# A gated-attention kernel with experts: GpSimd's arithmetic in the attention moved to VectorE and ScalarE

## The chip, the core and the metric

The kernel runs on one core of a Trainium2 chip. Its time is device time in microseconds, the median of several executions. Besides that there is one profiled execution, with the start and length of every instruction on each engine: TensorE (PE in the profile, PEld for its weight loads), VectorE (DVE), ScalarE (ACT), GpSimd (POOL) and SyncE (SP), which issues most of the transfers. Each engine works through its own queue of instructions in order and waits at semaphores for the others.

## The reference

Four sequences of 768 positions, eight heads of 48 channels, go through a linear attention whose state decays by a complex gate. After it a router sends each of the 3072 tokens to one of eight experts.

```python
mag = np.sqrt(a_re * a_re + a_im * a_im)
scale = np.minimum(mag, 0.999) / (mag + 1e-06)
a_re_n, a_im_n = (a_re * scale, a_im * scale)
for t in range(S):                       # S = 768
    new_re = ar * S_re - ai * S_im       # state: 48 x 48 for each batch and head
    new_im = ar * S_im + ai * S_re
    S_re, S_im = (new_re + kv, new_im)   # kv = outer product of k[t] and v[t]
    y[:, :, t] = np.einsum('bhd,bhde->bhe', q[:, :, t], S_re)
# experts, on x = y as (B*S, H*D) = (3072, 384)
logits = x @ w_gate                      # 8 experts
expert_idx = np.argmax(logits, axis=1)
h = np.maximum(x_sorted[lo:hi] @ w1[e], 0.0)     # 384 -> 1024
y_sorted[lo:hi] = h @ w2[e]                      # 1024 -> 384
return gate_w[:, None] * y
```

## The kernel before

**Two stages.** The attention takes chunks of 128 positions. A group g is one chunk of one batch (24 groups), a unit u is two groups (12 units), and four groups, one for each batch, make a step s of the sequence (6 steps). The experts follow: tokens are gathered by expert from a table in DRAM (`xs`), go through two matrix products, and are scattered to the output.

**What a unit computes.** The gate of each position is turned into a log magnitude and an angle; their running sums over a chunk come from a matmul with a triangular matrix.
- `decay_steps` (L226 to L250): ACT takes Ln of a_re (A) and Exp of its negative (R); the ratio of imaginary to real part replaces `ai` (L238); its square goes to R (L239); ACT takes Ln(1 + R), DVE forms A (L243), ACT an Exp, DVE the final A (L248).
- `decay_sums` (L269): matmul `csl` of A, then ACT makes E and Ei, the decay factor and its inverse, from PSUM.
- `angle_sums` (L298): matmul `cst` of the angles; DVE rounds it (r, L308), subtracts (f, L309) and takes the absolute value (fa, L312). `rotation` (L319) makes sine and cosine (CS) on ACT.
- `decayed` (L327): Qe = q * E and Ke = k * Ei (L333), for each group.
- `rotated` (L335): DVE multiplies these by CS into Q and K (L338).
- `scores` (L419): transposes of Q and K (tp), copies to SBUF (qt, kt; L78), scores (at), a mask (am, L438), and K^T v (dk).
- `outputs` (L448): y from the masked scores and from the state G, the new state t = dk + G (L468); once per step, all four G are t times the step's total decay M (L475). Then y goes to the expert table's rows (x) and to the router's logits.

**Routing.** Every other unit, `choose` and `route` (L352, L373) rank the tokens of four groups by expert, with some twenty DVE instructions on a few elements (L379 to L405, such as ov, rk, far, to). `put` (L407) then scatters the four groups' rows to `xs` by an indirect DMA, which GpSimd issues. `place` spreads these scatters over the units.

**Order.** The functions above are written down unit by unit with one unit's look-ahead (the gate of u + 1 beside the groups of u - 1). The order on each engine is then settled when the program is built, from dependences and estimated costs, so an instruction that moves to another engine can change the order on all. Two orders are fixed by hand: `act` chains the ACT activations in the order of the program, and `pool` does the same for GpSimd, with the scatters in the same chain:

```python
    def pool(ins):
        if "pool" in T:
            queue(ins, T["pool"])
        T["pool"] = ins
```

**Buffers that matter.** All `csl` and `cst` share one PSUM buffer (`psM`, bufs=1): each such matmul waits until the one before has been read, by E and Ei or by f. R, E and Ei have one buffer, Qe, Ke, Q and K two.

Of the kernel before, what the change touches and what calls it, by code (L numbers as in the profile page):

```python
# [13 lines left out]
AF = mybir.ActivationFunctionType  # L14
OP = mybir.AluOpType
# [14 lines left out]
def bc(ap, axis, n):  # L30

    shape = list(ap.shape)
    shape.insert(axis, n)
    return ap[tuple([slice(None)] * axis + [None])].to_broadcast(shape)
# [3 lines left out]
def kernel(  # L38
# [12 lines left out]
    nc = tc.nc  # L51
    B, H, S, D = q.shape
    DD = 2 * D
# [20 lines left out]
    def mm(o, lhsT, rhs, start=True, stop=True):  # L74
        return nc.tensor.matmul(o, lhsT=lhsT, rhs=rhs, start=start, stop=stop, skip_group_check=True)  # L75
# [10 lines left out]
    def const(shape, name, dt=FP):  # L86
        return cp.tile(shape, dt, name=name)
# [25 lines left out]
    gbuf = [const([P, H, DP], f"G{i}") for i in range(B)]  # L113
# [35 lines left out]
    T, W_T = {"put": []}, {}  # L149

    def queue(ins, before):

        tc.add_manual_dep(ins.ins, before.ins.name, NOSYNC, reason="queue order")
        return ins
# [32 lines left out]
    def act(**kw):  # L187

        ins = nc.scalar.activation(**kw)  # L189
        if "act" in T:  # L190
            queue(ins, T["act"])
        T["act"] = ins
# [6 lines that stand above are left out]
# [27 lines left out]
    def decay_steps(u):  # L226

        ar, ai = T["ar", u], T["ai", u]
        A = un.tile([P, W], FP, tag="A", name="A")
        R = un.tile([P, W], FP, tag="R", name="R", bufs=1)  # L230
        T["L", u], T["th", u] = A, ai

        def s0():
            act(out=A, in_=ar, func=AF.Ln)

        def s1():
            act(out=R, in_=A, func=AF.Exp, scale=-1.0)
            pool(nc.gpsimd.tensor_tensor(out=ai, in0=ai, in1=R, op=OP.mult))  # L238
            pool(nc.gpsimd.tensor_tensor(out=R, in0=ai, in1=ai, op=OP.mult))  # L239

        def s2():
            act(out=R, in_=R, func=AF.Ln, bias=1.0)
            nc.vector.scalar_tensor_tensor(out=A, in0=A, scalar=2.0, in1=R, op0=OP.mult, op1=OP.add)  # L243

        def s3():

            act(out=R, in_=A, func=AF.Exp, scale=-0.5, bias=ln2e6)
            nc.vector.scalar_tensor_tensor(out=A, in0=A, scalar=LN_CAP2, in1=R, op0=OP.min, op1=OP.subtract)  # L248

        return [s0, s1, s2, s3]  # L250
# [37 lines left out]
    def decay_total(s):  # L288

        mt = psL.tile([P, H, B], FP, tag="mm", padded_shape=[P, 128, B], name="mt")  # L290
        for h in range(H):
            nc.tensor.transpose(
                out=mt[0:DD, h], in_=T["er", s][:, h].rearrange("p a d -> p (a d)"), identity=ident[0:B, 0:B]
            )
        T["M", s] = un.tile([P, B, H], FP, tag="M", name="M")
        nc.scalar.copy(out=T["M", s][0:DD], in_=mt[0:DD].rearrange("p h b -> p b h"))
# [30 lines left out]
    def decayed(u, c):  # L327

        sl = slice(c * DM, (c + 1) * DM)
        for nm, src, dec in (("Q", "q", "E"), ("K", "k", "Ei")):  # L330
            e = T[nm, u, c] = ch.tile([P, H, D], FP, tag=nm + "e", name=nm + "e")
            o = e.rearrange("p h d -> p (h d)")
            pool(nc.gpsimd.tensor_tensor(out=o, in0=T[src, u][:, sl], in1=T[dec, u][:, sl], op=OP.mult))  # L333

    def rotated(u, c, nm):  # L335
        t = ch.tile([P, H, 2, D], FP, tag=nm, name=nm)
# [4 lines left out]
    def logits(xt, j):  # L341

        lt = psL.tile([P, P], FP, tag="mm", padded_shape=[P, 512], name="lt")
        for i in range(HP):
            mm(lt[32 * i : 32 * i + 32], wg[:, i], xt[:, i])
        ls = xl.tile([P, P], FP, tag="ls", name="ls")
        nc.scalar.copy(out=ls, in_=lt)
        lp = psL.tile([P, E], FP, tag="mm", padded_shape=[P, 512], name="lp")
        T["lp"] = mm(lp, ls, sel)
        nc.vector.tensor_copy(out=lg[:, j], in_=lp)  # L350
# [97 lines left out]
    def outputs(g):  # L448

        u, c = divmod(g, U)  # L450
        s, b = divmod(g, B)
        qts, ats = T.pop(("s", g))
        V, G = T["v", u][:, c], gbuf[b]
        y = psY.tile([P, HP, P], FP, tag="y", name="y")
        for i in range(HP):
            for z in range(2):
                hg, j = divmod(2 * i + z, 4)
                mm(y[z * DP : (z + 1) * DP, i], V[:, 2 * i + z], ats[hg][:, j], True, s == 0)
            if s > 0:
                for z in range(2):  # L460
                    hg, j = divmod(2 * i + z, 4)
                    mm(y[z * DP : (z + 1) * DP, i], G[0:DD, 2 * i + z], qts[hg][0:DD, j], False, True)
        if s < CB - 1:
            t = ch.tile([P, H, D], FP, tag="t", name="t")
            if s == 0:
                nc.scalar.copy(out=t[0:DD], in_=T["dk", g][0:DD])
            else:
                nc.vector.tensor_tensor(out=t[0:DD], in0=T["dk", g][0:DD], in1=G[0:DD, :, 0:D], op=OP.add)  # L468
            if b == B - 1:
                decay_total(s)  # L470
            T["t", b] = t
            if b == B - 1:
                for i in range(B):
                    M = bc(T["M", s][0:DD, i], 2, D)
                    pool(nc.gpsimd.tensor_tensor(out=gbuf[i][0:DD, :, 0:D], in0=T["t", i][0:DD], in1=M, op=OP.mult))  # L475
        xt = xl.tile([P, HP, P], FP, tag="xt", name="xt")
        nc.scalar.copy(out=xt, in_=y)
        tp = psB.tile([P, HP, 2, DP], FP, tag="tp", name="tpx")
        for i in range(HP):
            nc.tensor.transpose(out=tp[:, i].rearrange("p z d -> p (z d)"), in_=xt[:, i], identity=ident)  # L480
        if b == 0:
            T["x", g] = T["x"] = xl.tile([P, GR, XW], FP, tag="x", name="x", bufs=3)
        nc.scalar.copy(
            out=T["x"][:, b, :DM].rearrange("p (i z d) -> p i z d", z=2, d=D), in_=tp[:, :, :, 0:D]
        )
        logits(xt, g)
# [13 lines left out]
    for z in range(2):  # L500
        nc.sync.dma_start(
            out=wg[z * DP : z * DP + D, :, 0:E],
            in_=w_gate.rearrange("(i z d) e -> z d i e", z=2, d=D)[z],
# [12 lines left out]
    for u in range(NU + 1):  # L516
# [32 lines left out]
        for c in range(U):  # L549
            g = (u - 1) * U + c  # L550
            if g >= 0:
                scores(g)
            if u < NU:
                decayed(u, c)
            if g > 0:
                outputs(g - 1)
# [9 lines left out]
        if NU - 8 <= u < NU - 1:  # L566
            load_w(0, [u - (NU - 8)])
    outputs(NT - 1)
    for f in T["put"]:
        f()  # L570
# [301 lines left out]
```

## Time and profile before

| | before |
|---|---|
| time, median of 3 | 650.44 us (648.06 to 651.69) |
| span of the profiled execution | 648.4 us |
| attention | about 20 to 305 us |
| mean granted clock of TensorE | 0.962 |
| PE busy | 580.5 us (90%) |
| DVE busy | 252.0 us (39%) |
| ACT busy | 276.9 us (43%) |
| POOL busy | 209.2 us (32%) |

In the profile the first part is each engine's busy time. The second cuts the span into 40 slices of 16.2 us; a digit is the busy share in tenths, and PEclk is the clock that TensorE was granted, in tenths of full speed. A line of the timeline has start, length, engine, source line, operation, output and inputs with their shapes, and in brackets how long the engine had stood idle before it and who ended that. Every matmul has the line L75 and every plain copy L78, since helpers issue them: go by the names of the tiles. What GpSimd does in the attention:

| line | what | count | mean |
|---|---|---|---|
| L238 | ai = ai * R, 128x768 | 12 | 1811 ns |
| L239 | R = ai * ai, 128x768 | 12 | 1467 ns |
| L333 | Qe, Ke, 128x384 | 48 | 996 and 992 ns |
| L475 | G = t * M, 96x384 | 20 | 1111 ns |
| L408 | scatter to xs | 24 | 1025 ns |

### The profile page before, as it was taken

How to read it: one execution, taken by the hardware profiler on the slowest of the kernel's cores; microseconds unless marked ns; L12 is line 12 of the kernel's file. 1: busy time of each engine (PE TensorE's matmuls, PEld its weight loads, DVE VectorE, ACT ScalarE, POOL GpSimd, SP SyncE). 2: the span in 40 equal slices, each digit the busy share in tenths (PEclk: the TensorE clock that was granted, in tenths of full speed). 3: DMA queues.
4: the chain of work that ended last, by engine and by line, in shares of the span. 5: the costliest groups of instructions: out<-in, count | busy, mean ns of one | idle time of the engine just before them, and what ended most of it. 6: DMA issues, size and time to landing. Idle time of an engine off the chain costs nothing. (4 is left out here: it accounts for less than half of the span.)

```text
span 648.4 us, 8580 instructions
## 1 busy us (share of the span) xinstructions
PE 580.5 (90%) x3319; PEld 381.6 (59%) x3319; DVE 252.0 (39%) x499; ACT 276.9 (43%) x467; POOL 209.2 (32%) x192
## 2 busy tenths in 40 slices
PE   1497998998799699799989999999999999999993
PEld 0185776766668477587776555555555555555551
DVE  2355468567755758858231211212121021211210
ACT  5566774764564466475320115152341614225100
POOL 3444144174163444533211106032140512305111
PEclk9998889889799799899999999999999999999998
DMA  9979854653544525024303543736425373430000
GB/s 184 205 233 197 196 100 87 138 129 78 122 102 96 116 46 111 14 62 174 109 25 110 201 148 117 252 109 212 138 83 201 111 258 110 155 112 24 10 12 30
DMA packets 154233, 79.74 MB, mean 123 GB/s; under 512 B 130230, under 2 KB 145735, under 8 KB 154184
## 3 DMA queue, kind: packets, MB, share of 16 engines
q1 hardware_dynamic: 147008, 69.48, 41.8%
q0 software_dynamic: 3456, 9.47, 4.3%
q10 hardware_dynamic: 3720, 0.16, 0.3%
q8 instruction: 28, 0.46, 0.3%
q14 instruction: 21, 0.17, 0.1%
HBM read 63.74 MB, written 15.98 MB: 123 GB/s over the span
## 5 line engine op out<-in xcount | busy, mean ns | idle before, releaser
L75 PE MATMUL yps<-w2t,ht 128*128 128x384 f32 (+1 forms) x512 | 147.2, 488 | 0.3 <-DVE y L639 0.3
L75 PE MATMUL hps<-xt,w1t 128*128 128x448 f32 (+2 forms) x432 | 147.0, 500 | 0.0
L75 PEld LDWEIGHTS yps<-w2t,ht 128*128 128x128 f32 (+1 forms) x512 | 81.4, 177 | 64.5 <-issue 15.0
L75 PEld LDWEIGHTS hps<-xt,w1t 128*128 128x128 f32 x432 | 79.9, 190 | 61.6 <-issue 58.7
L624 ACT ACTIVATE ht<-hps 128x448 f32<-128x448 f32 (+2 forms) x36 | 18.1, 503 | 135.8 <-PE hps L75 135.8
L606 POOL DMA_INDIRECT out_dram<-y,xg x32 | 30.9, 966 | 94.2 <-DVE y L639 44.3
L639 DVE TENSOR_SCALAR y<-yps,xg 128x384 f32<-128x384 f32 x24 | 14.8, 617 | 118.4 <-PE yps L75 118.4
L628 DVE TENSOR_SCALAR ht<-hps 128x448 f32<-128x448 f32 (+2 forms) x36 | 20.6, 573 | 103.0 <-PE hps L75 103.0
L75 PEld LDWEIGHTS at<-qt,kt 96*128 96x128 f32 x384 | 52.7, 208 | 12.5 <-ACT kt L78 4.5
L75 PE MATMUL at<-qt,kt 96*128 96x128 f32 x384 | 57.7, 298 | 2.3 <-ACT kt L78 1.7
L677 POOL TENSOR_TENSOR cs<-cs,cw 128x768 f32<-128x768 f32 x12 | 21.7, 1805 | 117.4 <-ACT cw L673 117.4
L238 POOL TENSOR_TENSOR ai<-ai,R 128x768 f32<-128x768 f32 x12 | 21.7, 1811 | 115.2 <-ACT R L189 112.5
L75 PE MATMUL y<-am,v 128*64 128x128 f32 x384 | 52.4, 294 | 0.0
L75 PE MATMUL cst<-ai,tri_turn 128*128 128x384 f32 x48 | 26.3, 635 | 25.1 <-DVE f L309 22.6
L408 POOL DMA_INDIRECT xs<-x,to x24 | 24.6, 1025 | 73.2 <-DVE x L404 31.3
L438 DVE TENSOR_TENSOR am<-at,tri 128x512 f32<-128x512 f32 x48 | 33.0, 688 | 38.8 <-PE at L75 38.7
L75 PE MATMUL y<-qt,G 96*64 96x128 f32 x320 | 45.2, 283 | 0.0
L75 PE MATMUL csl<-A,tri_half 128*128 128x384 f32 x48 | 25.2, 613 | 19.8 <-DVE A L248 17.2
L75 PEld LDWEIGHTS y<-am,v 128*64 128x64 f32 x384 | 33.0, 140 | 13.2 <-issue 8.2
L430 PE MATMUL tp<-ident,Q 128*96 128x128 f32 x192 | 34.7, 297 | 2.9 <-DVE Q L338 1.6
L75 PE MATMUL dk<-v,K 128*96 128x48 f32 x320 | 34.1, 261 | 3.4 <-DVE t L468 3.4
L78 ACT COPY qt<-tp 96x512 f32<-96x512 f32 x48 | 27.0, 580 | 21.1 <-PE tp L430 20.6
(122 smaller groups left out, 829.0 us busy)
## 6 DMA issues: line engine op xcount, KB each, us to landing
w1t<-in_moe_w_dram SPq DMA_DIRECT2D x7, 1536.0 KB
w2t<-in_moe_w_dram SPq DMA_DIRECT2D x7, 1536.0 KB
xs<-zrow SPq DMA_DIRECT2D x7, 772.0 KB
ar<-in_a_re_dram SPq DMA_DIRECT2D x12, 384.0 KB
ai<-in_a_im_dram SPq DMA_DIRECT2D x12, 384.0 KB
q<-in_q_dram SPq DMA_DIRECT2D x12, 384.0 KB
k<-in_k_dram SPq DMA_DIRECT2D x12, 384.0 KB
v<-in_v_dram SPq DMA_DIRECT2D x12, 384.0 KB
```

The source lines that it names most:

```text
L75: return nc.tensor.matmul(o, lhsT=lhsT, rhs=rhs, start=start, stop=stop, skip_group_check=True)
L78: (nc.scalar.copy if i % 2 else nc.vector.tensor_copy)(out=o, in_=in_)
L238: pool(nc.gpsimd.tensor_tensor(out=ai, in0=ai, in1=R, op=OP.mult))
L408: pool(nc.gpsimd.indirect_dma_start(out=xs[:, :], out_offset=bass.IndirectOffsetOnAxis(ap=to[:, i : i + 1], axis=0), in_=x[:, i], in_offse ...
L430: nc.tensor.transpose(out=tp[0:DD, j], in_=X[:, hg * 4 + j], identity=ident)
L438: nc.vector.tensor_tensor(out=am, in0=at, in1=bc(tri, 1, 4), op=OP.mult)
L606: return nc.gpsimd.indirect_dma_start(out=out, out_offset=bass.IndirectOffsetOnAxis(ap=idx, axis=0), in_=y[0:m], in_offset=None, bounds_ch ...
L624: relu = nc.scalar.activation(out=ht[:, f], in_=ps, func=AF.Relu)
L628: nc.vector.tensor_scalar(out=ht[:, f], in0=ps, scalar1=0.0, scalar2=None, op0=OP.max)
L639: nc.vector.tensor_scalar(out=y, in0=ps, scalar1=gate, scalar2=None, op0=OP.mult)
L677: nc.gpsimd.tensor_tensor(out=s, in0=s, in1=w, op=OP.add)
```

## The change

All four kinds of arithmetic leave GpSimd. The ratio, the products for Qe and Ke, and the state decay go to VectorE; the square becomes a Square activation on ScalarE, inside the chain of activations. GpSimd keeps the scatters of the attention, and its two instructions of the range check beside the experts are left as they are. The aim is to free VectorE and GpSimd from each other, to shorten the steps that GpSimd took, and to let the scatters go without waiting in a queue of arithmetic.

```diff
         def s1():
             act(out=R, in_=A, func=AF.Exp, scale=-1.0)
-            pool(nc.gpsimd.tensor_tensor(out=ai, in0=ai, in1=R, op=OP.mult))
-            pool(nc.gpsimd.tensor_tensor(out=R, in0=ai, in1=ai, op=OP.mult))
+            nc.vector.tensor_tensor(out=ai, in0=ai, in1=R, op=OP.mult)
+            act(out=R, in_=ai, func=AF.Square)
...
-            pool(nc.gpsimd.tensor_tensor(out=o, in0=T[src, u][:, sl], in1=T[dec, u][:, sl], op=OP.mult))
+            nc.vector.tensor_tensor(out=o, in0=T[src, u][:, sl], in1=T[dec, u][:, sl], op=OP.mult)
...
-                    pool(nc.gpsimd.tensor_tensor(out=gbuf[i][0:DD, :, 0:D], in0=T["t", i][0:DD], in1=M, op=OP.mult))
+                    (nc.vector.tensor_tensor(out=gbuf[i][0:DD, :, 0:D], in0=T["t", i][0:DD], in1=M, op=OP.mult))
```

The instruction order changes with it. On VectorE, in a unit that routes, the new order is: Qe and Ke of the first group, x, ai (L238), ov, rk, far, far, am, to, Qe and Ke of the second group, r, f, r, A (L243), f, am, fa, A (L248). On ScalarE the Square stands between Exp (R) and the second pair of E and Ei. On TensorE the next unit's first `csl` comes after the second `cst`, with half a group of transposes and eight or nine y products between them.

## The prediction

> **What bounds the kernel now.** I read the page's first two parts, then the busy time of each engine in stretches of a few microseconds, then the waits of the attention, and last the timelines of VectorE (DVE) and GpSimd (POOL) at the places where TensorE (PE) stood still. The page first:
>
> ```profile
> PE 580.5 (90%) x3319; PEld 381.6 (59%) x3319; DVE 252.0 (39%) x499; ACT 276.9 (43%) x467; POOL 209.2 (32%) x192
> ...
> PE   1497998998799699799989999999999999999993
> DVE  2355468567755758858231211212121021211210
> POOL 3444144174163444533211106032140512305111
> PEclk9998889889799799899999999999999999999998
> ```
>
> The attention fills slices 1 to 19 (about 20 to 305 us); the experts after it have PE at 9 throughout. So only the attention can change. There PE is mostly busy but has dips, DVE stands at 5 to 8, and the granted clock falls to 7 or 8 in the slices with a dip. One dip in stretches of 2 us (columns: PE, PEld, DVE, ACT, POOL, clock, DMA):
>
> ```profile
> 157.00:159.00 2.00, 2.00 (x21) 1.16 (x21) 1.76 (x5) 0.34 (x1) 1.77 (x3) 1.00 0.01 2
> 159.00:161.00 2.00, 0.88 (x14) 0.64 (x10) 1.97 (x2) 1.94 (x4) 1.97 (x3) 1.00 0.35 74
> 161.00:163.00 2.00, 0.00 (x0) 0.00 (x0) 2.00 (x1) 0.00 (x0) 2.00 (x3) 0.82 1.18 213
> 163.00:165.00 2.00, 0.01 (x1) 0.01 (x1) 1.87 (x4) 0.00 (x0) 0.65 (x1) 0.50 0.08 8
> 165.00:167.00 2.00, 2.00 (x5) 1.39 (x6) 0.32 (x1) 0.00 (x0) 0.00 (x0) 0.50 0.03 8
> 167.00:169.00 2.00, 2.00 (x12) 1.96 (x11) 2.00 (x4) 0.86 (x2) 0.00 (x0) 0.50 0.62 126
> ```
>
> PE and ACT stop altogether, DVE is "busy" with one instruction, and PE then runs some 5 us at half clock. The DVE and POOL timelines say which instruction, and PE's what it waited for:
>
> ```profile
> 157.55 1.10 DVE L396 TENSOR_SCALAR ov<-rk 128x4 f32<-128x4 f32 x1
> ...
> 159.08 4.60 DVE L401 TENSOR_TENSOR far<-far,ov 128x4 f32<-128x4 f32 x1
> 163.72 0.16 DVE L403 SCALAR_TENSOR_TENSOR to<-far,rk 128x4 int32<-128x4 f32 x1
> 163.79 0.55 DVE L308 TENSOR_SCALAR r<-cst 128x384 f32<-128x384 f32 x1
> ```
> ```profile
> 159.82 1.00 POOL L333 TENSOR_TENSOR Qe<-q,E 128x384 f32<-128x384 f32 x1
> 160.76 1.00 POOL L333 TENSOR_TENSOR Ke<-k,Ei 128x384 f32<-128x384 f32 x1
> 161.72 0.99 POOL L333 TENSOR_TENSOR Qe<-q,E 128x384 f32<-128x384 f32 x1
> 162.66 0.98 POOL L333 TENSOR_TENSOR Ke<-k,Ei 128x384 f32<-128x384 f32 x1
> ```
> ```profile
> 164.99 1.65 PE L75 MATMUL cst<-ai,tri_turn 128*128 128x384 f32 x2 [5.11 <-DVE f L309]
> ```
>
> A DVE instruction on four elements per partition, 0.16 us elsewhere, lasts 4.60 us and ends just when POOL's run of four products ends. Behind it in DVE's queue stand r and f, which PE's second cst needs. In the waits of 20 to 305 us this is PE's main named loss:
>
> ```profile
> PE cst L75 <- DVE f L309: 22.6, 11, 5.1
> PE csl L75 <- DVE A L248: 3.6, 1, 3.6
> PE dk L75 <- DVE t L468: 3.4, 3, 1.1
> ```
>
> The same place comes once in each unit that routes: at 105, 158, 212 and 265 us.
>
> **What the Trainium skill says.** "SBUF — State Buffer", section Who interferes with whom: a DVE instruction with two SBUF inputs contends with a GpSimd instruction that reads SBUF, and the loser waits for the whole instruction. The trace agrees: 4.60 us for 0.16 us of work, four back-to-back POOL instructions long. "TensorE: Matmul & The Clock Gate", Part 1: after an idle window of about 3.4 us the clock halves. The trace agrees: 0.50 after 5.1 us of idleness. "VectorE: DVE Perf Modes", the errata section: an fp32 tensor_tensor lasts (N+151)/0.96 ns. That is 0.56 us for 384 elements and 0.96 us for 768; the trace has 0.55 (L309, L468) and 0.96 (L243).
>
> **The change part by part.**
> - L238 (angle ratio, 12 times): 1.81 us on POOL becomes about 0.96 us on DVE (L243's row).
> - L239 (its square, 12 times): 1.47 us on POOL becomes a Square on ACT, about 0.84 us (128x768 ACTIVATE rows of 0.83 to 0.85; the Square of L673 has 0.83).
> - L333 (decayed Q and K, 48 times): 0.99 us on POOL becomes 0.55 us on DVE.
> - L475 (state decay, 20 times): 1.11 us on POOL becomes about 0.55 us on DVE (L468, 96x384). One operand is broadcast; L338, also with one, has 0.95 against 0.96, so I add nothing for it.
>
> POOL loses all 109 us of work beside DVE in the attention; DVE gains 12 x 0.96 + 48 x 0.55 + 20 x 0.55 = 49 us, ACT 10 us. DVE loses its stalls: L401 is 15.0 us for 6 x 0.16, L396 4.4 for 6 x 0.17, and L397, L400 and L248 show some 3 us over their usual times: about 20 us. DVE thus goes from 184 us in the attention to about 213.
>
> Gain A, the four routing stalls. In the changed kernel's order DVE has, between the rank (L395) and r: x 0.16, ai 0.96, ov, rk, far, far 0.7, am 0.69, to 0.16, Qe and Ke 1.1: 3.8 us, against 6.2 now (157.55 to 163.79). PE's idleness of 5.1 us shrinks by about 2.5 to 3, to below what halves the clock, and the roughly 6 us at half clock (163 to 169), worth 3 us, go with it. So 5.7 us each, 4 x 5.7 = 23 us.
>
> Gain B, the decay chain. ACT waits 20.3 us, ten times, for POOL's R (L239). Two steps of 3.3 us become 0.96 + 0.84 = 1.8 us. But the Square now stands in ACT's queue in front of the second E and Ei (L276, L277), which the first cst waits for through the one PSUM buffer, and ACT waits there for DVE's ai. I count half of the 1.5 us, in 11 units: 8 us.
>
> Gain C, the state update. It lasts 3.53 + 1.47 us on POOL in each of five rounds and four times 0.55 = 2.2 on DVE; little of PE's time hangs on it (dk behind t: 3.4 us): 3 us.
>
> Cost D, a fuller DVE queue. In the new order csl (next unit) follows the second cst after only some 2.1 us of PE work (half a group of transposes, eight or nine y products), while DVE needs r, A (L243), f, am, fa and A (L248), 4.2 us, before csl may start (in the units with the state update r, K, f, A: 3.1 us). That is a wait of 1 to 2 us per unit; behind csl stand the next at and tp. Less than a full unit's 2 us everywhere, since early units have fewer PE instructions: about 1 us x 11 = 11 us. The other new DVE work lies beside PE and ACT work: per unit DVE comes to about 18 us in a unit of 24.
>
> Sum: 23 + 8 + 3 - 11 = 23; 650.4 - 23 = 627 us. The start (DMA share near 1 until 50 us) and the experts stay; the scatters alone on POOL leave earlier, but each needs DVE's index or gate first, and they are hidden.
>
> **The rivals.**
> - The new order costs nothing (D is zero, because PE's own queue covers it): 34 us gained, 616 us; if clock dips outside the four stalls (slices at 8 before 100 us) also go, down to 606. For it: PE's waits other than cst's are small now. Against it: DVE's queue gets 49 us longer.
> - Half a gain: the routing stretch on DVE keeps PE idle over 3.4 us, and the clock still halves; A is only 2.5 x 4 = 10, B, C and D as above: 10 us, 640 us. For it: 3.8 us of DVE work in one piece, in front of r.
> - Slower: DVE becomes the bound. If half of its new 49 us stand in PE's way (24), and A brings only its idle part (10 to 12), B and C nothing, it ends 12 us slower, 662. For it: each unit's r, f, fa, A and the products for Q and K all pass one in-order queue. Against it: 213 us in 260 to 285 leave a fifth to a quarter of it free, and stalls of 20 us are gone for certain.
> - No change: gains of A and losses of D cancel, about 650.
>
> **How the numbers follow.** Likeliest, 627 (617 to 636): 0.45. D nothing or less: 0.25. Half gain: 0.16. No change: 0.04. Slower: 0.10. So faster 0.86, same 0.04, slower 0.10. Range: from 608, which takes in most of the D-nothing case, to 644, which takes in the half gain; outside are the full clock at the low end (about 0.06) and no change and slower (0.14).
>
> **What would show it.** Right: L401 and L396 at 0.16 us; no gaps of 5 us before the second cst; the clock at 1.0 where POOL used to run; DVE near 210 us before the experts, who start some 23 us earlier and last as before. The L333 and L475 products at 0.55, L238 at 0.96. D right: new PE waits of 1 to 2 us on A (L248) before csl. Wrong: PE waits on DVE in every unit that sum to more than now, ACT waiting for ai longer than it did for POOL, or products on DVE longer than 0.6 us.

## The result and the profile after

| | before | after |
|---|---|---|
| time, median of 4 runs | 649.73 us (648.06 to 651.69) | 621.82 us (620.54 to 622.01) |
| span of the profiled execution | 648.4 us | 618.8 us |
| mean granted clock of TensorE | 0.962 | 0.988 |
| first expert product (`hps`) starts at | 328.3 us | 297.5 us |

The ratio of after to before is 0.9565, with a 95% interval of 0.9534 to 0.9597. A few executions ran longer at a lower granted clock than the others of their kernel; the ratios leave them out, and only_state below, with three of four such, has no usable ratio. Of the 29.6 us between the two spans, the attention brings 30.8 and the experts give 1.2 back. The page's first two parts, after:

```profile
PE 563.5 (91%) x3319; PEld 369.7 (60%) x3319; DVE 264.6 (43%) x579; ACT 284.5 (46%) x479; POOL 104.0 (17%) x100
...
PE   1498799899899899998899999999999999999993
...
DVE  2567787787787779781312112121121211211111
...
POOL 1000000100200200302120042140521405214011
PEclk9999999999999999999799999999999999999997
```

PE has the same 3319 matmuls in 17 us less of busy time, since a matmul at half clock is busy for longer (the second pair of `cst` took 1.65 us at a clock of 0.50 in the prediction's line; at full clock such a pair takes 0.88). PEclk has lost its dips of the attention and has a new one in slice 19, where the experts begin. DVE holds 80 instructions more, which take 48.9 us, but only 12.6 us more busy time: some 25 us of stalls are gone, and records of neighbouring instructions overlap a little, which busy time counts once. The dip that the prediction showed has this counterpart, again in stretches of 2 us:

```profile
147.00:149.00 2.00, 2.00 (x21) 1.83 (x18) 1.89 (x6) 1.60 (x4) 0.00 (x0) 1.00 0.37 75
149.00:151.00 2.00, 2.00 (x21) 1.11 (x21) 1.35 (x5) 0.90 (x3) 0.00 (x0) 1.00 0.84 139
151.00:153.00 2.00, 1.90 (x20) 1.39 (x19) 0.96 (x3) 1.92 (x5) 0.00 (x0) 1.00 1.14 230
```

PE (first column after the length) hardly pauses, POOL (fifth) is empty, and the clock stays at 1.00. In the same place, DVE's timeline:

```profile
147.72 0.16 DVE L396 TENSOR_SCALAR ov<-rk 128x4 f32<-128x4 f32 x1
...
148.31 0.16 DVE L401 TENSOR_TENSOR far<-far,ov 128x4 f32<-128x4 f32 x1
...
149.16 0.55 DVE L333 TENSOR_TENSOR Qe<-q,E 128x384 f32<-128x384 f32 x1
149.63 0.55 DVE L333 TENSOR_TENSOR Ke<-k,Ei 128x384 f32<-128x384 f32 x1
150.83 0.56 DVE L308 TENSOR_SCALAR r<-cst 128x384 f32<-128x384 f32 x1 [0.65 <-PE cst L75]
```

L401 took 4.60 us before and takes 0.16 now. Before `r`, DVE now even waits 0.65 us for PE. What PE still waits for up to 285 us, where the attention's last units run:

```profile
PE tp L430 <- DVE Q L338: 6.8, 5, 1.5
PE csl L75 <- DVE A L248: 5.8, 9, 3.5
PE y L75 <- DVE am L438: 3.4, 5, 0.8
PE cst L75 <- DVE f L309: 3.0, 4, 1.2
```

The wait of `cst` for f has fallen from 22.6 us to 3.0; others on DVE have grown.

**A ledger for all runs.** From 20 us to the first expert product, one line of the windows view gives length, PE's busy time and clock. Here for before, then after:

```profile
20.00:328.20 308.20, 268.64 (x2276) 208.79 (x2277) 192.45 (x367) 179.63 (x307) 123.31 (x110) 0.93 0.53 119
```
```profile
20.00:297.30 277.30, 249.76 (x2275) 195.47 (x2275) 203.03 (x442) 184.98 (x314) 22.69 (x20) 0.99 0.59 132
```

Length less PE busy is idle time: 39.6 and 27.5 us. One minus the clock (0.928 and 0.993 unrounded), times the length, is what the clock cost: 22.2 and 1.9. The rest is work at full clock: 247 and 248. It stays at 246 to 252 us in every kernel below (262 in the one with added matmuls), so a kernel's time is this work, plus idle, plus clock. Two limits of this ledger: where PE is idle while the clock is halved, the time stands in both columns (2.7 us in before, 1.9 in ratio_only, about 1 in after and decay_stays, less elsewhere). And the clock's record begins only at 37 to 41 us. Up to there a `cst` matmul takes 0.85 us against 0.49 later, so PE ran at not much over half speed; about 6 us of this are part of the "work" of every kernel (5.5 to 7.0).

The table has this ledger and, as "DVE stalls", what DVE instructions took above the shortest of their own line and shape, where that is more than 0.1 us. Each row is one profiled execution, and executions differ: in the largest group, before ran with mean clocks of 0.960 to 0.978 and took 644 to 650 us. Each group of runs had runs of before beside it, with medians of 647 to 649 us.

| kernel | median us | `hps` starts | PE idle | lost to the clock | DVE stalls, the most at |
|---|---|---|---|---|---|
| before | 647 to 650 | 328.2 | 40 | 22.2 | 24.9, L401 14.1 |
| ratio_only | 650.2 | 328.5 | 42 | 20.5 | 24.1, L400 12.9 |
| only_state | not used | 321.7 | 40 | 11.9 | 26.5, L381 9.1 |
| rank_psum | 639.3 | 315.2 | 35 | 8.5 | 14.8, L243 8.2 |
| warm12 | 639.0 | 316.6 | 29 | 5.5 | 24.8, L396 12.8 |
| only_products | 638.0 | 316.8 | 31 | 17.1 | 19.2, L381 10.4 |
| square_only | 628.5 | 308.0 | 35 | 3.4 | 22.3, L381 11.6 |
| decay_stays | 626.3 | 304.1 | 25 | 11.3 | 22.0, L333 14.6 |
| after | 621.8 | 297.3 | 28 | 1.9 | 0 |
| both_dve | 621.4 | 298.0 | 22 | 6.8 | 20.2, L381 8.9 |
| after_early | 618.4 | 296.5 | 26 | 0 | 0 |
| only_decay | 617.2 | 295.3 | 27 | 1.7 | 8.7 |
| state_stays | 617.0 | 294.0 | 25 | 0 | 3.0 |
| products_stay | 616.2 | 292.2 | 25 | 0 | 16.4, L475 6.7 |

### The profile page after: what moved, and what is told of

The parts are those of the page before. It is cut to its first block, busy times and chain, and to the rows that moved or that the text cites. A ratio compares the mean times of both kernels' runs of the same rounds, so it can differ in the third digit from the quotient of the medians.

```text
span 618.8 us, 8535 instructions
## 1 busy us (share of the span) xinstructions
PE 563.5 (91%) x3319; PEld 369.7 (60%) x3319; DVE 264.6 (43%) x579; ACT 284.5 (46%) x479; POOL 104.0 (17%) x100
## 5 line engine op out<-in xcount | busy, mean ns | idle before, releaser
L408 POOL DMA_INDIRECT xs<-x,to x24 | 26.6, 1107 | 284.4 <-DMA fl<-f 109.4
L639 DVE TENSOR_SCALAR y<-yps,xg 128x384 f32<-128x384 f32 x24 | 14.8, 617 | 118.4 <-PE yps L75 118.4
L75 PE MATMUL at<-qt,kt 96*128 96x128 f32 x384 | 53.5, 282 | 0.8 <-ACT kt L78 0.7
L75 PEld LDWEIGHTS at<-qt,kt 96*128 96x128 f32 x384 | 47.9, 192 | 10.2 <-DVE kt L78 3.1
L75 PE MATMUL y<-am,v 128*64 128x128 f32 x384 | 50.6, 285 | 3.5 <-DVE am L438 3.4
L75 PE MATMUL y<-qt,G 96*64 96x128 f32 x320 | 42.9, 278 | 0.0
L75 PE MATMUL csl<-A,tri_half 128*128 128x384 f32 x48 | 24.2, 590 | 20.5 <-DVE A L248 17.9
L75 PEld LDWEIGHTS y<-am,v 128*64 128x64 f32 x384 | 31.6, 135 | 14.4 <-issue 7.7
L78 ACT COPY qt<-tp 96x512 f32<-96x512 f32 x48 | 27.5, 583 | 21.5 <-PE tp L430 21.3
L430 PE MATMUL tp<-ident,K 128*96 128x128 f32 x192 | 30.8, 279 | 1.5 <-DVE K L338 1.5
L75 PE MATMUL dk<-v,K 128*96 128x48 f32 x320 | 32.2, 253 | 0.0
```

Source lines behind the costliest of these rows:

```text
L78: (nc.scalar.copy if i % 2 else nc.vector.tensor_copy)(out=o, in_=in_)
L408: pool(nc.gpsimd.indirect_dma_start(out=xs[:, :], out_offset=bass.IndirectOffsetOnAxis(ap=to[:, i : i + 1], axis=0), in_=x[:, i], in_offse ...
L430: nc.tensor.transpose(out=tp[0:DD, j], in_=X[:, hg * 4 + j], identity=ident)
L639: nc.vector.tensor_scalar(out=y, in0=ps, scalar1=gate, scalar2=None, op0=OP.mult)
```

## The experiments

The theory from the prediction is that DVE's stall behind POOL's products holds PE up and then halves its clock. Against it stand the length of the decay step (two slow POOL instructions in it), and the order: where POOL's work falls in each unit.

### One part alone, and all but one part

The change has three parts: decay (L238, L239), products (L333) and state (L475). Each was made alone on the kernel before (only_...) and undone alone in the kernel after (..._stays).

only_products:
```diff
-            pool(nc.gpsimd.tensor_tensor(out=o, in0=T[src, u][:, sl], in1=T[dec, u][:, sl], op=OP.mult))
+            nc.vector.tensor_tensor(out=o, in0=T[src, u][:, sl], in1=T[dec, u][:, sl], op=OP.mult)
```


> Only the products for Qe and Ke (L333) go to DVE; ratio, square and state decay stay on GpSimd. Theory: GpSimd's run of four products is what stalls DVE, so most of the 28 us is here: 628 to 636, L401 under 1 us. Rival (each part brings its share of the shorter chain): about a third, 640.

Measured: 637.95 us, ratio 0.9834 (0.9788 to 0.988): outside what the theory said, and close to the rival's third (640). L401 is at 0.16 us, the gaps of 5 us are gone, but the clock still costs 17.1 us. The stall moved to L381 (cx) and to the products themselves, now on DVE: at 154.35 us two cx instructions take 1.85 us together and the next 1.32 while POOL runs L238 (1.80) and L239 (1.47) from 154.19 us. Removing POOL work from one place does not free DVE where other POOL work remains.

only_decay:
```diff
-            pool(nc.gpsimd.tensor_tensor(out=ai, in0=ai, in1=R, op=OP.mult))
-            pool(nc.gpsimd.tensor_tensor(out=R, in0=ai, in1=ai, op=OP.mult))
+            nc.vector.tensor_tensor(out=ai, in0=ai, in1=R, op=OP.mult)
+            act(out=R, in_=ai, func=AF.Square)
```


> Only ratio and square (L238, L239) leave GpSimd; products and state decay stay there. Theory: the run of four products remains, so L401 or a neighbour still lasts 2 us or more on average, and little is gained: 640 to 650. Rival (chain, since this is the step that ACT waited for): 630 to 638.

Measured: 617.21 us, ratio 0.9519 (0.9475 to 0.9562), far below both expectations. POOL keeps all 48 products, and yet L401 is at 0.16 us in all six places. POOL's timeline of this kernel in a unit that routes shows why:

```profile
142.11 1.00 POOL L333 TENSOR_TENSOR Qe<-q,E 128x384 f32<-128x384 f32 x1 [5.81 <-ACT E L189]
143.08 1.71 POOL L333 TENSOR_TENSOR Ke<-k,Ei 128x384 f32<-128x384 f32 x1
148.17 1.00 POOL L333 TENSOR_TENSOR Qe<-q,E 128x384 f32<-128x384 f32 x1 [3.39 <-DVE am L438]
149.13 1.00 POOL L333 TENSOR_TENSOR Ke<-k,Ei 128x384 f32<-128x384 f32 x1
```

The run of four products has become two pairs, 3.4 us apart, and L401, at 145.31 us, falls between them.

products_stay and state_stays, on the kernel after:
```diff
-            nc.vector.tensor_tensor(out=o, in0=T[src, u][:, sl], in1=T[dec, u][:, sl], op=OP.mult)
+            pool(nc.gpsimd.tensor_tensor(out=o, in0=T[src, u][:, sl], in1=T[dec, u][:, sl], op=OP.mult))
```
```diff
-                    (nc.vector.tensor_tensor(out=gbuf[i][0:DD, :, 0:D], in0=T["t", i][0:DD], in1=M, op=OP.mult))
+                    pool(nc.gpsimd.tensor_tensor(out=gbuf[i][0:DD, :, 0:D], in0=T["t", i][0:DD], in1=M, op=OP.mult))
```


> The changed kernel with the products for Qe and Ke (L333) back on GpSimd. Theory: DVE instructions with two SBUF inputs stall again for up to 4 us in the units that route, the clock dips come back: 636 to 648. Rival (chain): the ratio and square are short and off GpSimd, 622 to 630.

> The changed kernel with the state decay (L475) back on GpSimd. The parts do not add: with ratio and square off GpSimd the rest is worth nothing, so 616 to 623. If the state decay on DVE is worth what it brought together with the products (11 us between only_products and decay_stays): 630 to 634.

Measured: products_stay 616.22 us, ratio 0.9513 (0.9481 to 0.9545), the lowest median of all, where the theory had it among the slow ones and the rival, too, expected more (622 to 630); state_stays 616.97 us, 0.9494 (0.9416 to 0.9573), as foretold. The windows view of products_stay, up to its first expert product:

```profile
20.00:292.20 272.20, 247.53 (x2276) 194.85 (x2277) 198.40 (x397) 186.29 (x317) 72.08 (x66) 1.00 0.61 135
```

POOL is busy for 72 us and DVE has 16.4 us of stalls, but PE has a clock of 1.00 and less idle time than in the kernel after. So the products did not have to move. It reaches the experts 5.1 us earlier than after does. At the same transposes of `xt` (tpx) it is 2.9 us ahead at 208 us and 2.3 us ahead at 287 us; the rest comes at the handover to the experts (see after_early below). What gained the first part was not traced.

decay_stays (products and state moved, decay left on POOL) and only_state:

> The changed kernel with ratio and square back on GpSimd; the products and the state decay stay on DVE. If moving ratio and square is what brings the gain, and the rest almost nothing, 634 to 642. If the products and the state decay bring most when they move together, 622 to 630.

> Only the state decay (L475) goes to DVE. The ratio, the square and the four products stay on GpSimd back to back, so the stall of L401 or a neighbour stays: 642 to 650. If the state update is what costs (PE waits for dk behind t): 632 to 640.

Measured: decay_stays 626.26 us, 0.9661 (0.9611 to 0.9711), in the second range: products and state bring more when they move together. only_state is inconclusive (ratio 1.0152, from 1.0031 to 1.0274); the one execution that counts took 643.8 us. Together: none of the parts 647, products 638, decay 617, products and state 626, decay and products or decay and state 616 to 617, all three 622. The parts don't add. Decay alone brings 30 us, products alone 9, and on top of decay neither brings anything that can be told from noise.

### The stall without the change: rank_psum

The ranking's small tiles rk and far go to PSUM, so that none of the four instructions from ov to the second far (L396 to L401) has two SBUF inputs. PE, ACT and POOL keep exactly the order of before; on DVE a small instruction of the ranking changes places with its neighbour in a few spots.

```diff
-        ps = psL.tile([P, n + 1, E], FP, tag="mm", padded_shape=[P, 64, E], name="rps")
+        ps = psL.tile([P, n + 3, E], FP, tag="mm", padded_shape=[P, 64, E], name="rps")
...
-        rk = xl.tile([P, n], FP, tag="rk", name="rk")
+        rk = ps[:, n + 1, 0:n]
...
-        far = xl.tile([P, n], FP, tag="far", name="far")
+        far = ps[:, n + 2, 0:n]
```


> The kernel before, with the rank and its distance (rk, far) kept in PSUM, so that ov, rk, far and far (L396 to L401) have at most one SBUF input each; GpSimd keeps all its arithmetic, and the order on every engine is that of before. Theory (the stall behind GpSimd's products is the main cost): L401 falls from 2.5 us to about 0.2 us, the 5 us gaps before the second cst fall to 1 or 2 us, the clock stays up in these units, and it gains 12 to 20 us (630 to 638), unless the next DVE instruction with two SBUF inputs, A (L243), takes over the stall. Rival (the gain is that of shorter steps once GpSimd is out of the chain): under 4 us gained, 646 to 650.

Measured: 639.3 us (636.46 to 647.89), ratio 0.9866 (0.9798 to 0.9934). L401 fell from 2.51 us on average to 0.16, but the gain is 8 us, not the whole: the exception that the expectation named came true. The DVE timeline in the third routing unit of this kernel:

```profile
253.91 0.56 DVE L309 TENSOR_TENSOR f<-cst,r 128x384 f32<-128x384 f32 x1
254.39 4.54 DVE L243 SCALAR_TENSOR_TENSOR A<-A,R 128x768 f32<-128x768 f32 x1
```

r and f now pass, and the next DVE instruction with two SBUF inputs, A (0.95 us elsewhere), takes the wait. This is the cleanest evidence for the mechanism: with POOL's work and the order of the other engines unchanged, the place of two small tiles moved the stall. It agrees with what the Trainium skill says in "SBUF — State Buffer", section Who interferes with whom: outside the 2-port modes a DVE instruction with at most one SBUF input doesn't contend, one with two does. One input alone is no safe sign, though: L396 (ov) reads only rk, and with rk in SBUF it lasted 4.24 us behind the products in warm12. The page names tensor_scalar, which L396 is, among the operations that can enter a 2-port mode; that L396 was in one, no run here shows. PE's gaps over 2 us fell from 21.0 to 6.6 us in sum and the clock's cost from 22.2 to 8.5.

### The clock by itself: warm12

Twelve matmuls of the identity follow the first `cst` of each later routing unit, so that PE isn't idle while DVE stalls. They write to a spare part of the tile, and nothing reads them.

```diff
-        cs = psM.tile([P, DM], FP, tag="mm", padded_shape=[P, 512], name="cst")
-        mm(cs, tri_turn, T["th", u][:, sl])
+        ct = psM.tile([P, 512], FP, tag="mm", name="cst"); cs = ct[:, 0:DM]
+        mm(cs, tri_turn, T["th", u][:, sl]); [mm(ct[:, DM:], ident, ident) for _ in range(12) if c == 0 and u >= 4 and u % 2 == 0]
```


> The kernel before, with twelve idle matmuls (128x128, into unused columns of the PSUM buffer) behind the first cst of each unit that routes; nothing reads them, all results stay. They fill about 2.7 us of the 5.1 us in which PE waits there for DVE, and make no wait shorter. If the halved clock after the gap is a loss of its own: the clock stays up in these units, the clock lost in the attention falls by 8 to 12 us, 637 to 644. If only the waiting counts: no change, 646 to 652.

Measured: 639.04 us (637.28 to 641.5), ratio 0.9831 (0.9749 to 0.9913). PE's timeline at the second routing stall:

```profile
152.65 2.84 PE L75 MATMUL cst<-ident 128*128 128x128 f32 x24
...
159.15 0.88 PE L75 MATMUL cst<-ai,tri_turn 128*128 128x384 f32 x2 [1.39 <-DVE f L309]
```

Four such rows, the first at 104.43 us, are 11.4 us of work for nothing. DVE's stalls are as long as before (24.8 us), but the clock's cost up to the experts falls by 16.7 us, and the kernel gains some 10 us, in the range of the first expectation. Of the 16.7 us, 10.2 belong to the routing units; most of the rest was lost elsewhere, as from 60 to 70 us, ahead of the first added matmul. Another 2.9 us are lost to the clock after the first expert product. The second `cst` takes 0.88 us, where the prediction's line had 1.65. So the halved clock is a loss of its own beside the wait. The order changed somewhat with the added matmuls, so the 10 us aren't theirs to the last one. "TensorE: Matmul & The Clock Gate", Part 1, in the Trainium skill, has the clock fall after an idle window of about 3.4 us, and this run agrees; the last section has falls without such a window.

### The decay step taken apart: ratio_only, square_only, both_dve

On the kernel before, only L238 went to DVE, only L239 to ACT (as a Square), or both to DVE:

```diff
-            pool(nc.gpsimd.tensor_tensor(out=ai, in0=ai, in1=R, op=OP.mult))
+            nc.vector.tensor_tensor(out=ai, in0=ai, in1=R, op=OP.mult)
```
```diff
-            pool(nc.gpsimd.tensor_tensor(out=R, in0=ai, in1=ai, op=OP.mult))
+            act(out=R, in_=ai, func=AF.Square)
```


> Only the ratio (L238) goes to DVE; its square and all else stay on GpSimd. ACT's order is all but that of before, and the step between Exp (R) and Ln falls from 3.3 to about 2.5 us. Length of the chain as cause: about half of what moving both brings, 630 to 636. Order as cause (the Square in ACT's queue lets copies fill ACT's wait): little, 640 to 648.

> Only the square (L239) goes to ACT; the ratio and all else stay on GpSimd. The step is about 2.7 us, hardly shorter than in ratio_only, but ACT's queue has the Square and the copies around it as in the changed kernel. Length of the chain: 632 to 640. Order: nearly all, 617 to 626.

> Ratio and square both go to DVE, none to ACT. The step is as short as in the changed kernel (about 1.9 us), but ACT has no Square, and waits between Ei and Ln as before. Length of the chain: 617 to 624. Order: 630 to 642.

Measured: ratio_only 650.21 us, 1.0056 (1.0033 to 1.0079), above both expectations; square_only 628.47, 0.9693 (0.9641 to 0.9745), between its two; both_dve 621.37, 0.958 (0.9522 to 0.9639), as the length of the chain would have it. In ratio_only the decay step is some 0.8 us shorter, the order almost that of before, and the stall is still there, on the next instruction of the ranking. DVE's timeline of this kernel:

```profile
158.32 4.46 DVE L400 TENSOR_TENSOR far<-tid,rk 128x4 f32<-128x4 f32 x1
162.70 0.54 DVE L309 TENSOR_TENSOR f<-cst,r 128x384 f32<-128x384 f32 x1
```

f waits behind it as before, and nothing is gained: this much off the step is worth nothing by itself. square_only keeps almost all of before's stalled time, but at L381, at the start of the ranking:

```profile
149.34 2.90 DVE L381 TENSOR_TENSOR cx<-cx,oh 128x8 bf16<-128x8 bf16 x2
152.31 0.19 DVE L393 TENSOR_TENSOR ro<-rps,oh 128x32 f32<-128x32 f32 x1
```

There only the ranking's own matmul waits for it: PE's waits on L381 are 6.5 us in four places, none over 1.8, and the clock costs 3.4 us instead of 22.2. So almost the same stalled time goes with a kernel that is 19 us faster, where it stands in front of other work. both_dve speaks against the idea that the Square on ACT is what sets a better order, for it does nearly as well without it.

What stays open: square_only and both_dve differ from before in the order of all engines as well as in the length of the step. How the gain of decay divides between the shorter step and the new position of POOL's runs was not separated; POOL work put back into the kernel after at chosen places, with the order held, was not tried.

### The handover to the experts: after_early

In the kernel after, PE waits at the end, and runs at half clock for the first expert products. PE's timeline, and the windows view around it:

```profile
292.90 0.39 PE L75 MATMUL lp<-sel,ls 128*128 128x8 f32 x2 [0.44 <-ACT ls L347]
295.77 1.95 PE L595 MATMUL tp<-ident,xg 128*128 128x128 f32 x6 [2.49 <-DMA xg<-xs]
```
```profile
283.00:305.00 22.00, 17.52 (x135) 13.64 (x134) 6.55 (x32) 4.38 (x11) 2.91 (x3) 0.84 0.13 43
```

The gather of the first expert's tokens follows the scatters to `xs`. In the kernel before the attention ended so late that this gather wasn't waited for. The experiment ranks the second-last four groups one group earlier:

```diff
-        else:
-            table("natural_log_exp_and_others")
-            choose(NT - 2 * GR, GR)()
-            T["put"] += route(NT - 2 * GR, False)
+        elif T["put"]:
...
+            if g == NT - 2 * GR + GR:
+                table("natural_log_exp_and_others")
+                choose(NT - 2 * GR, GR)()
+                T["put"] += route(NT - 2 * GR, False)
```


> The changed kernel with the routing of groups 16 to 19 written one group earlier. In the changed kernel the experts' first gather waits for these scatters: PE stands 2.5 us and runs some 3 us at half clock. If that is a real loss: 3 to 4 us less than the changed kernel, 617 to 619. If the scatters end no earlier, or the attention gives it back: 621 to 624.

Measured: 618.42 us (618.16 to 619.84), ratio 0.9529 (0.945 to 0.9608). The median is 3.4 us below that of after, as expected, but the interval takes in the ratio of after (0.9565). The wait for the gather is gone, and the clock stayed at 1.000. That this came from earlier scatters is not shown. The last scatter before the gather leaves only 0.2 us earlier:

```profile
288.08 0.97 POOL L408 DMA_INDIRECT xs<-x,to  x1 [2.38 <-DMA xs<-x,to]
```
```profile
287.87 0.97 POOL L408 DMA_INDIRECT xs<-x,to  x1 [2.62 <-DMA xs<-x,to]
```

The first line is from after, the second from after_early. In after this scatter took 4.7 us to land, so that the gather left at 292.8 us; in after_early it took 2.6 us. Why that one landing was slow stays open. PE also comes to the gathered tokens 2.0 us later in after_early (295.3 against 293.3 us), so the first expert product starts only 0.9 us earlier, and 1.5 us more come from the experts, which now begin at full clock. products_stay and state_stays don't have the wait either: their last scatter before the end leaves at 284.4 and 286.2 us, against 288.1 in the kernel after.

## Why the prediction was right, and where its sum was off

The time of 621.8 us lies in the range, 5 us under the 627 predicted. The direction holds, and so does the mechanism: DVE instructions stalled behind POOL kept `cst` waiting, and the clock fell after it. What freed `cst` is another part than the expectations had it, and several terms of the sum had another size and cancelled in part. That the total came within 5 us is to that extent luck.

- **Instruction costs.** L333 0.55 us, L475 0.55, L238 0.95, Square 0.84 to 0.85, L401 and L396 0.16: all as worked out. DVE's attention came to about 203 us up to the first expert product, against 210.
- **Gain A, the wait: 10 to 12 us foretold, 17.4 measured.** The four gaps before the second `cst` (2.37, 5.11, 5.11 and 4.79 us) are gone altogether. The prediction left 2 to 2.5 us in each, for 3.8 us of DVE work before `r`; in the trace after, that work was done before PE needed it. It also counted 5.1 us in each place, where the first had 2.37: at 105 us DVE got in between the products (last section). And the 4.60 us of L401 are not the four products alone (3.83 us from 159.82): L401 started at 159.08, while POOL still issued a scatter (L408, 158.78 to 159.79).
- **Gain A, the clock: 12 us foretold, 20.3 measured. This is the mis-sized term.** The prediction counted the clock after the four routing stalls only, and these spells did cost 11.9 us by its count, half of their length. Another 10.2 us were lost after shorter gaps: 59.9 to 70.1 us (5.1), and 83.8 to 87.2, 138.4 to 141.8 and 193.0 to 196.4 (1.7 each). The prediction took an idle window of about 3.4 us for what halves the clock, and none of these spells had one before it; it had part of them in its low rival alone. They vanished too. (PE was idle in part of the spells, so 2.7 of the 22.2 us before and about 1 of the 1.9 after are counted as idle time as well: without these the clock's gain is 18.8 us.)
- **Gain B, the decay chain: 8 us foretold, about 2 seen.** PE's wait of `cst` for f fell by 19.6 us, of which the four gaps are 17.4; little is left for a shorter step, and ratio_only gained nothing from 0.8 us off it. What moving the decay did, as only_decay shows, is to take the stall away from `cst`; the prediction's reading and the expectations gave that to the products. Whether the shorter step or the new order did it was not separated.
- **Gain C, the state update: 3 us foretold.** The wait of `dk` for t, 3.4 us, is gone.
- **Cost D, the fuller DVE queue: 11 us foretold, about 11 measured, elsewhere.** `csl` waits for A 5.8 us instead of 3.6: once 3.5 us at the start, as before, and eight times some 0.3, not 1 to 2. But `tp` waits for Q 6.8 instead of 1.6, and `y` for am, not among the largest waits before, 3.4: 2.2 + 5.2 + 3.4 = 10.8. The place was wrong, so that the size agrees is luck.
- **Not foreseen: the handover.** The gather is waited for 2.5 us, and the experts take 1.2 longer, since the spell at half clock (293.6 to 300.4 us) reaches into them and costs 1.5 us there.

The rival with D at nothing foretold 616 us, and 606 with the other dips gone as well; the dips went, and D was paid. Half a gain, no change and slower are out: no gap of 5 us is left, and the clock's record is 1.00 from its first entry at 37.6 us up to 293.6.

## What to carry to other kernels

In these runs a GpSimd instruction beside VectorE cost what stood behind the stalled VectorE instruction in its queue, not its own time and not the stall's: find the matmul that waits, and look for whatever separates the two, which may be another instruction than the one stalled on (here two decay steps, and not the 48 products). Where parts share one stall, test each part alone and each left out: here versions that move only some of the parts have medians of 616 to 617 us, and moving all of them is not faster (622 us; 3 to 5 us behind by the ratios, 0.949 to 0.952 against 0.957, whose intervals overlap). And price PE's pauses twice, as idle time and as halved clock, short clusters too, but don't count idle time at half clock in both.

## What was unexpected of the hardware

The clock fell not only after a gap of 5 us. Before, PE had gaps of 1.57 us (from 56.4) and 1.24 us (from 58.8), and then, by the windows view:

```profile
60.00:64.00 4.00, 3.94 (x14) 3.29 (x15) 2.26 (x5) 2.01 (x4) 2.34 (x3) 0.50 0.64 223
64.00:68.00 4.00, 4.00 (x30) 3.43 (x28) 2.21 (x4) 3.85 (x6) 0.00 (x0) 0.50 1.03 341
```

This spell lasts ten microseconds (59.9 to 70.1 us), after 2.8 us of idleness in two pieces. In state_stays the clock is halved from 294.0 us without a gap of more than 0.73 us in the 10 us before. In square_only a gap of 1.76 us in front of the ranking's matmul was followed by half clock at 152.7 and 248.3 us, but the same gap at 199.28 us was not. The unit with half clock at 152.7 us, and then the one without, in stretches of 3.4 us:

```profile
149.30:152.70 3.40, 1.64 (x22) 1.19 (x19) 3.23 (x5) 2.08 (x4) 3.23 (x4) 1.00 0.16 58
152.70:156.10 3.40, 3.40 (x27) 3.07 (x24) 1.84 (x6) 0.84 (x1) 1.41 (x2) 0.50 0.12 24
```
```profile
197.10:200.50 3.40, 2.18 (x22) 1.74 (x21) 3.30 (x4) 1.19 (x2) 3.21 (x4) 1.00 0.22 71
200.50:203.90 3.40, 2.87 (x36) 2.59 (x36) 2.94 (x10) 1.73 (x4) 2.41 (x3) 1.00 0.05 11
```

The stretches are not chosen freely. Within each of the 14 traces, the changes of the clock lie whole multiples of 3.41 us apart. With PE's busy share counted on this grid, from 40 to 300 us and where the clock was full, all 24 stretches with less than 46% were followed by half clock, 26 of 93 with 46 to 67%, and none of 885 with more. So here PE's work in a fixed stretch goes with the fall better than the length of one gap does: the gap at 199.28 us was divided by the grid and left 64% and 84%. What decides in the middle range stays open.

A run of POOL instructions back to back held DVE through all of it in three routing units of before (4.60 us) and at L243 in rank_psum (4.54). In the first routing unit of before it did not. There DVE got in once for each product; the four products end at 106.23, 107.20, 108.15 and 109.10 us:

```profile
105.48 0.78 DVE L396 TENSOR_SCALAR ov<-rk 128x4 f32<-128x4 f32 x1
106.30 0.92 DVE L397 SCALAR_TENSOR_TENSOR rk<-fst,rk 128x4 f32<-128x4 f32 x1
107.25 0.92 DVE L400 TENSOR_TENSOR far<-tid,rk 128x4 f32<-128x4 f32 x1
108.21 0.92 DVE L401 TENSOR_TENSOR far<-far,ov 128x4 f32<-128x4 f32 x1
```

What made the difference is not shown.
